# First heads loaded in fp32 and cast by VectorE, attention outputs copied out of PSUM at once, and zero matmuls without a bank of their own

## The chip, the cores and the metric

One core of a Trainium2 chip. The metric is the time of one execution in device microseconds (us); lower is better. Times are medians of several executions. A ratio is the mean time of one kernel's fast runs over the mean time of the other's fast runs of the same rounds on the same chip, so it is not quite the ratio of the medians quoted beside it. Profiles are of one execution each, and their span is about 1.8 us shorter than the time of the same execution.

## The reference

Eight batches, twelve heads, 448 rows, head width 64. Attention uses a sigmoid in place of the softmax; its output goes through a token mixer and a channel mixer with residuals.

```python
scores = scale * np.matmul(q, k.transpose(0, 1, 3, 2)) - np.log(S)
attn = 1.0 / (1.0 + np.exp(-scores))
x = np.matmul(attn, v)                       # then heads side by side: (8, 448, 768)
h = np.maximum(x.transpose(0, 2, 1) @ w_tok1, 0.0) @ w_tok2
u = x + h.transpose(0, 2, 1)
out = u + np.maximum(u @ w_ch1, 0.0) @ w_ch2
```

## The kernel before

The kernel is written as a plan. Every operation is declared with a guessed duration; a scheduler on the host picks an order for each engine from those guesses, and the instructions are emitted in that order. The order in each engine's list is then fixed, so a changed guess in one place can move instructions far away.

Batch 0 has a pipeline of its own, because nothing else can run yet: load q and k of four heads (a "unit", m = 0, 1, 2), turn them with TensorE transposes, score matmuls (qk), sigmoid on ScalarE, value matmuls (xa), copy to xT, transpose (xb), lay out as x, token mixer (k, then h), token result, eviction to uT. When all of uT is there, the first channel matmul (c<-uT) can start. From then on TensorE has work from the mixer of one batch and the attention of the next.

Loads cast fp32 to fp16 and are issued by GpSimd:

```python
for hs in [(0, 1)] if m or what == "v" else [(0,), (1,)]:
    def emit(hs=slice(hs[0], hs[-1] + 1)):
        for s in range(2):
            nc.gpsimd.dma_start(
                out=t[64 * s : 64 * s + 64, hs, :, :].rearrange("r h j e -> r h (j e)"),
                in_=view[s, :, hs, :],
            )
```

Zero matmuls keep TensorE occupied during the start-up. Nine come first ("up"), single ones ("fill") go where the plan sees TensorE idle between 4 and 21 us. All write one PSUM bank called idle:

```python
def run_up():
    for _ in range(9):
        nc.tensor.matmul(out=idle[:, :], lhsT=uT[0][:, 0, 0:128], rhs=uT[0][:, 0, :], start=True, stop=True)
# ...
def emit():      # a filler
    nc.tensor.matmul(out=idle[:, 0:256], lhsT=uT[0][:, 0, 0:128], rhs=uT[0][:, 0, 0:256], start=True, stop=True)
```

The token result of batch 0 is accumulated onto the attention output, which therefore stays in its PSUM banks until the end:

```python
nc.tensor.matmul(out=ps[s](every), lhsT=h1[0][...], rhs=w_tok2[:, t, 0:J, :],
                 start=False, stop=(t == 1), skip_group_check=True)
# ... and then one copy PSUM -> uT
```

## Time and profile before

Median 380.89 us (380.54 to 380.92, three runs).

| | before |
|---|---|
| span of the profile | 378.7 us |
| first score matmul, first sigmoid | 7.61, 8.03 us |
| end of batch 0's last sigmoid | 31.07 us |
| first channel matmul | 41.53 us |
| from there to the end | 337.2 us |

The page of the kernel before: the span, the share of the engines, and two rows of the table of 40 slices, one digit a slice (tenths of the slice that TensorE was busy, and tenths of full clock granted to it). PE is TensorE, PEld its weight loads, DVE VectorE, ACT ScalarE, POOL GpSimd; in the columns of the other views, L439 is line 439 of the kernel and a q after the name, as in SPq, is that engine's DMA queue.

```profile
span 378.7 us, 7932 instructions
PE 370.8 (98%) x3243; PEld 191.3 (51%) x3243; DVE 160.6 (42%) x296; ACT 205.7 (54%) x252; POOL 118.5 (31%) x265
...
PE   8999999999999999999999999999999999999994
...
PEclk9999999999999999999999999999999999999999
```

TensorE is the limit nearly everywhere. Its timeline at the start (columns: start in us, duration in us, engine, line, operation, output<-inputs, shapes, count):

```profile
1.16 3.54 PE L439 MATMUL idle<-uT 128*128 128x448 f16 x9 [1.16 <-DVE uT L432]
4.64 0.94 PE L499 MATMUL tk<-ident,k 128*64 128x128 f16 x7
5.51 0.61 PE L452 MATMUL idle<-uT 128*128 128x256 f16 x4
6.05 0.58 PE L499 MATMUL tq<-ident,q 128*64 128x128 f16 x7
6.56 0.61 PE L452 MATMUL idle<-uT 128*128 128x256 f16 x4
7.10 0.58 PE L499 MATMUL tk<-ident,k 128*64 128x128 f16 x7
7.61 0.57 PE L542 MATMUL qk<-qT,kT 64*64 64x448 f16 x4
```

The chain of waits of the kernel before, from batch 0's last sigmoid to the first channel matmuls (start, duration, what):

```profile
30.07 1.01 ACT attn L557
...
31.12 0.41 PE xa L579 x4
...
36.32 0.76 PE xa L693 x3
...
37.75 0.55 ACT uT L708
...
41.60 1.24 PE c L871 x6
```

So before 41.6 us the limit is the start-up chain, after it TensorE.

### The profile page before, as it was taken

Reading aid. Unit: us, or ns where it says so; the run is one execution under the profiler, and the core shown is the slowest. Engines: PE = TensorE matmul, PEld = TensorE weight load, DVE = VectorE, ACT = ScalarE, POOL = GpSimd, SP = SyncE. Lnnn points to the kernel's source line nnn. Section 1 sums busy time; section 2 is a strip of 40 time slices with the busy share of each in tenths; the row PEclk is TensorE's granted clock in tenths of the full one; section 3 lists DMA queues with packets and bytes.
Section 4 is the critical chain, followed back from the end, with each engine's and each line's share of the span. In section 5 each row is a group of like instructions: output and inputs, shape, how many; then the busy total and the mean of one; then the engine's idle time right before and its main releaser. Section 6 shows DMA issues by size and latency. Waiting matters only on the chain.

```text
span 378.7 us, 7932 instructions
## 1 busy us (share of the span) xinstructions
PE 370.8 (98%) x3243; PEld 191.3 (51%) x3243; DVE 160.6 (42%) x296; ACT 205.7 (54%) x252; POOL 118.5 (31%) x265
## 2 busy tenths in 40 slices
PE   8999999999999999999999999999999999999994
PEld 4555544555445554445444555444445655555662
DVE  3444434644344323453355313643432365754221
ACT  2987884486757766787678466846664130200000
POOL 9973326344344434444344343430000000000000
PEclk9999999999999999999999999999999999999999
DMA  6999999989987999999999999991103553300353
GB/s 80 181 176 205 208 210 176 153 141 184 146 126 111 174 162 235 146 120 208 190 149 161 162 180 156 145 197 39 30 16 97 113 106 94 73 2 0 85 123 85
DMA packets 98804, 50.56 MB, mean 134 GB/s; under 512 B 72336, under 2 KB 95120, under 8 KB 98768
## 3 DMA queue, kind: packets, MB, share of 16 engines
q0 software_dynamic: 24400, 21.93, 44.2%
q1 hardware_dynamic: 74368, 28.13, 40.8%
q8 instruction: 25, 0.41, 0.4%
q14 instruction: 11, 0.09, 0.1%
HBM read 43.84 MB, written 11.01 MB: 145 GB/s over the span
## 4 chain that ended last, share of the span: by engine, by line
PE 90%; POOL 4%; DMA 2%; ACT 1%; DVE 1%; issue 0%; POOLq 0%
PE c L871 30%; PE c L916 25%; PE qk L542 10%; PE xa L579 8%; PE yn L794 5%; PE k L764 5%; PE c L925 4%; DMA k<-in_k_dram 2%; POOL k L304 1%; POOL q L304 1%; POOL v L304 1%; ACT attn L557 1%; POOL w_tok L337 1%; PE xa L693 1%; PE tk L499 0%
## 5 line engine op out<-in xcount | busy, mean ns | idle before, releaser
L557 ACT ACTIVATE attn<-qk,att_bias 128x896 f16<-128x896 f32 (+1 forms) x172 | 160.9, 987 | 78.6 <-PE qk L542 78.3
L871 PE MATMUL c<-uT,w_ch 128*128 128x448 f16 x576 | 118.0, 353 | 0.1
L916 PE MATMUL c<-w_ch,h2aT 128*128 128x384 f16 x576 | 98.5, 326 | 0.0
L896 DVE TENSOR_SCALAR h2aT<-c 128x448 f16<-128x448 f32 x96 | 59.9, 624 | 77.4 <-PE c L871 77.2
L871 PEld LDWEIGHTS <-w_ch 128*128 128x128 f16 x576 | 53.4, 98 | 56.7 <-issue 11.6
L916 PEld LDWEIGHTS <-h2aT 128*128 128x128 f16 x576 | 55.2, 98 | 40.1 <-issue 4.5
L940 DVE TENSOR_TENSOR u<-u,c 128x384 f32<-128x384 f32 x48 | 26.6, 554 | 77.4 <-PE c L916 77.4
L542 PE MATMUL qk<-qT,kT 64*64 64x448 f16 x672 | 53.1, 363 | 0.2 <-ACT uT L708 0.2
L579 PE MATMUL xa<-attn,v 64*64 64x448 f16 x672 | 36.5, 350 | 0.4 <-ACT attn L557 0.4
L728 POOL COPY mark<-attn 1x1 f16<-1x1 f16 x54 | 9.6, 178 | 80.0 <-ACT attn L557 79.9
L823 ACT ACTIVATE u<-u 128x768 f16<-128x768 f32 x21 | 17.8, 846 | 25.0 <-DVE u L815 25.0
L542 PEld LDWEIGHTS <-kT 64*64 64x64 f16 x672 | 14.5, 104 | 29.8 <-issue 26.9
L815 DVE TENSOR_TENSOR u<-x,yn 128x384 f32<-128x384 f16 x48 | 24.9, 548 | 9.1 <-PE yn L794 9.1
L475 POOL COPY kp<-k 128x384 f16<-128x384 f16 (+1 forms) x54 | 21.2, 427 | 21.0 <-DMA k<-in_k_dram 16.0
L794 PE MATMUL yn<-h,w_tok 128*128 128x384 f16 x128 | 27.4, 328 | 0.0
L579 PEld LDWEIGHTS <-v 64*64 64x64 f16 x672 | 19.6, 107 | 13.2 <-issue 1.6
L612 ACT ACTIVATE xT<-xa 128x448 f16<-128x448 f32 x43 | 21.1, 547 | 9.3 <-PE xa L579 8.1
L475 POOL COPY qp<-q 128x384 f16<-128x384 f16 (+1 forms) x54 | 21.3, 430 | 9.0 <-DMA q<-in_q_dram 8.7
L764 PE MATMUL k<-x,w_tok 128*128 128x384 f16 x112 | 20.6, 327 | 0.1
L776 DVE TENSOR_SCALAR h<-k 128x384 f16<-128x384 f32 x28 | 15.4, 556 | 11.9 <-PE k L764 10.8
L315 POOL DMA_DIRECT2D k<-in_k_dram x21 | 15.0, 716 | 7.4 <-issue 5.9
L794 PEld LDWEIGHTS <-w_tok 128*128 128x128 f16 x128 | 11.0, 98 | 12.1 <-issue 5.9
(57 smaller groups left out, 186.7 us busy)
## 6 DMA issues: line engine op xcount, KB each, us to landing
out_dram<-u SPq DMA_DIRECT2D x48, 192.0 KB, 3.0
k<-in_k_dram POOLq DMA_DIRECT2D x21, 224.0 KB, 5.2
q<-in_q_dram POOLq DMA_DIRECT2D x21, 224.0 KB, 5.5
v<-in_v_dram POOLq DMA_DIRECT2D x21, 224.0 KB, 5.4
w_ch<-in_moe_w_ch_dram POOLq DMA_DIRECT2D x6, 768.0 KB, 15.9
out_dram<-ut SPq DMA_DIRECT2D x8, 192.0 KB, 3.2
v<-in_v_dram POOLq DMA_DIRECT2D x6, 112.0 KB, 4.7
x<-xT SPq DMA_TRANSPOSE x36, 4.6
```

The lines of the kernel that those rows point to most:

```text
L475: nc.gpsimd.tensor_copy(out=pm[:, to, :, :], in_=src[:, fr, :, :])
L542: nc.tensor.matmul(out=ps[64 * s : 64 * s + 64, h, 0:S], lhsT=kT[64 * h : 64 * h + 64, i, s, :], rhs=qT[64 * h : 64 * h + 64, :, s, :], st ...
L557: nc.scalar.activation(out=at[:, hs, :], in_=ps[:, hs, 0:S], func=SIGMOID, bias=bias_t[:, :], scale=att_scale,)
L579: nc.tensor.matmul(out=ps[s](slice(64 * h, 64 * h + 64)), lhsT=vf[64 * s : 64 * s + 64, h, order[i], :], rhs=attn[i][64 * s : 64 * s + 64, ...
L612: nc.scalar.activation(out=xt[:, s, c0 : c0 + S], in_=ps[s](every), func=COPYF)
L764: nc.tensor.matmul(out=ps[:, :], lhsT=w_tok1[:, w1_slot(side, blk), 128 * t : 128 * t + 128], rhs=X[b][:, x_block(side, blk), c], start=(b ...
L794: nc.tensor.matmul(out=ps[:, :], lhsT=w_tok2[:, t, s0 : s0 + 2, :], rhs=h1[b][:, t, c], start=(t == 0), stop=(t == 1),)
L815: nc.vector.tensor_tensor(out=to, in0=x, in1=y, op=ADD)
L871: nc.tensor.matmul(out=to(), lhsT=w_ch1[cb // 4][:, db, 128 * (cb % 4) : 128 * (cb % 4) + 128], rhs=uT[b][:, db, :], start=(db == 0), stop ...
L896: nc.vector.tensor_scalar(out=h2aT[b][:, cb, :], in0=to(), scalar1=0.0, scalar2=None, op0=MAX)
L916: nc.tensor.matmul(out=ps[:, :], lhsT=h2aT[b][:, cb, 128 * blk : 128 * blk + 128], rhs=w, start=(cb == 0), stop=(cb == NCB - 1),)
L940: nc.vector.tensor_tensor(out=t, in0=t, in1=ps[:, :], op=ADD)
```

## The change

Its intent is to reach the first channel matmul sooner. The first heads of q and k come as plain fp32 copies on the hardware queues of SP and ScalarE and are cast by VectorE, which saves two pairs of GpSimd issues and should start the sigmoids earlier. Batch 0's attention outputs are copied out of PSUM at once; the token result gets its own bank and VectorE adds x to it, so that banks come free and the units overlap. Fillers take a bank only for a moment. Around it: six zero matmuls at the start instead of nine, batch 1's keys and queries loaded ahead of the channel weights, batch 1's transposes no longer held back until batch 0's last uT evictions (`hold`), and evictions of the first two units that a late-bound variable had sent to ScalarE by mistake (`last` in a closure) back on VectorE. The core of the diff:

```diff
-    FILL = 21.0
+    FILL, UP = 21.0, 6
...
+                if m == 0 and hs == (0,):
+                    first = const(f"{what}_first", [128, J, E], FP32)
+                    def fetch(first=first):
+                        for s, queue in enumerate((nc.sync, nc.scalar)):
+                            queue.dma_start(
+                                out=first[64 * s : 64 * s + 64, :, :].rearrange("r j e -> r (j e)"),
+                                in_=view[s, :, 0, :],
+                            )
+                    def cast(first=first):
+                        nc.vector.tensor_copy(out=t[:, 0, :, :], in_=first[:, :, :])
+                    o = op(f"fetch_{what}", "SQ", 2.4 if what == "q" else 0.5, fetch, uses=[first])
+                    yield op(f"cast_{what}", "DVE", 0.32, cast, [o], [first, t], rank=-2)
+                    continue
...
-        for _ in range(9):
+        for _ in range(UP):
...
+        spot = bank(f"fill_{fill['n']}", [128, 256])
         def emit():
             nc.tensor.matmul(
-                out=idle[:, 0:256], lhsT=uT[0][:, 0, 0:128], rhs=uT[0][:, 0, 0:256], start=True, stop=True
+                out=spot[:, :], lhsT=uT[0][:, 0, 0:128], rhs=uT[0][:, 0, 0:256], start=True, stop=True
             )
...
-        hold = uT_ops[0][-2:] if b == 1 and m else []
+        hold = []
...
+                    tile_ = bank(f"kt_{b}_{m}_{s}", [128, S])
...
-                            start=False,
+                            start=(t == 0 and not last),
...
+                    if not last:
+                        nc.vector.tensor_tensor(out=y, in0=xt[:, s, 0:S], in1=to(every), op=ADD)
```

(Cut: the split of the first key eviction between ScalarE and VectorE, the table load moved ahead, load orders, priorities of the plan, a rule that holds token groups back when a value group is due.)

## The prediction

Short names in it: SWDGE are the loads that GpSimd issues, HWDGE those on the hardware queues of SP and ScalarE; K1 and KT are the two matmul steps of batch 0's token mixer; ch1_1 and ch1_2 are pieces of the channel weights.

> **What bounds it now.** From 41.6 us to about 346 us the chain of waits is almost nothing but matmul groups, and by the stage table TensorE is busy 29.2 of 29.3 us and then 100%: it is bound by TensorE there, and the change removes no real matmul from that stretch. What can be won lies in the start-up before the first channel matmul (41.6 us). The timeline shows three parts of it:
> 1. Filling: the first score matmul is at 7.61 us, the first sigmoid at 8.03. SWDGE issues of k/q (1.04 to 1.20 us a pair, one pair after another on GpSimd) land some 3.2 us after issue.
> 2. ScalarE: batch 0's sigmoids run from 8.03 to 31.08. They are worth about 20.7 us; 2.3 us go to waits and to other work on ScalarE (x evictions of 0.60, relus of 0.38).
> 3. Tail: last sigmoid 31.08 to last uT eviction 38.30, 7.2 us, strictly serial (xa, xT, xb, x, K1, h, KT, uT). Then 3.3 us of batch-1 transposes and scores.
>
> **What the change does.** The first q and k go in fp32 on SP and ScalarE queues; VectorE casts them. Two SWDGE pairs (2.24 us of GpSimd issue) disappear, so later loads are issued about 2.2 us earlier. The Trainium skill ("DMA: Bandwidth & Descriptors", SWDGE vs HWDGE) says a casting DMA must come from GpSimd, hence the VectorE cast. Its "Latency and other measured facts" gives 0.6 us to the first byte on hardware queues against 1 us; no load of this trace uses one, but output stores do: about 0.59 us to issue, 2.6 to 3.0 to land. ScalarE's own k issue stands behind the table load (1.28 us) and the tiny sigmoid, so I expect q landed at about 3.2 and k at 4 to 5.2, first score 5.5 to 6.5, first sigmoid about 6.2: gain 1.8 us.
>
> Batch 0's xa is copied out at once and the token result gets its own bank with x added on VectorE. By the instruction order, two x evictions (0.60 each), two relus and one uT eviction leave ScalarE. Estimate: sigmoids last 21.5 instead of 23.05 us; last one ends near 27.8. The tail stays about 7.3 us (the last unit is built as before), but batch 1's transposes are now inside it. First channel group at about 35.3 to 35.8 instead of 41.6, with two scores fewer done by then (about 0.7 us). So 6 − 0.7 ≈ 5.3 us, all on the critical path. Removed fillers (21 zero matmuls) filled idle slots: no gain.
>
> DMA is near saturation (1.25 of its share, 204 GB/s) from 28 to 60 us. Batch 1's six k/q loads now precede the first channel weight: 672 KB more, about 3.3 us at that rate, against 2.2 us earlier issue. I estimate it landed near 31 to 32 us, before 35; ch1_1 near 36, ch1_2 near 41, still ahead of use.
>
> **Prediction: 375.6 us** (1.4% faster), range 373.3 to 378.3. Faster by over 2%: 0.10; within 2%: 0.88; slower: 0.02.
>
> **What would show it.** Right: first sigmoid near 6.2 us; batch 0's last sigmoid near 28; first channel matmul near 35.5; from there to the end the same length as before (337 us) within 1 us.
>
> **What would make it wrong.** k on ScalarE's queue landing after 5.5 us; PE idle between the six zero matmuls and k, so the granted clock drops below 1.0 in the first slices; first channel matmul waiting for its weight or for batch 1's k/q (TensorE waits in order); VectorE, which takes over the work, delaying xT/h; or batch 1 becoming ScalarE-bound, so that the early start is given back before 70 us.

## The result, and the profile after

| | before | after |
|---|---|---|
| median | 380.88 us (six runs) | 382.38 us (380.96 to 383.12, six runs) |
| ratio | | 1.0036, 95% interval 1.0016 to 1.0056 |
| span of the profile | 378.7 us | 380.9 us |
| first sigmoid | 8.03 us | 7.53 us |
| end of batch 0's last sigmoid | 31.07 us | 32.92 us |
| first channel matmul | 41.53 us | 41.28 us |
| from there to the end | 337.2 us | 339.7 us |

The change did not gain 5.3 us; it lost about 1.5.

The page of the changed kernel, the same lines:

```profile
span 380.9 us, 7888 instructions
PE 370.5 (97%) x3222; PEld 189.2 (50%) x3222; DVE 163.0 (43%) x303; ACT 205.5 (54%) x249; POOL 115.4 (30%) x261
...
PE   6999999999999999999899999999999999999994
PEclk9599999999999999999999999999999999999999
```

The second slice of the clock row reads 5. The stage table shows it more closely (columns: stretch, its length, then busy us and number of instructions of PE, PEld, DVE, ACT and POOL, granted clock, DMA share, GB/s):

```profile
6.00:8.00 2.00, 1.50 (x22) 0.98 (x23) 1.29 (x3) 0.85 (x2) 2.00 (x5) 0.99 0.96 129
8.00:12.00 4.00, 4.00 (x43) 2.27 (x40) 1.79 (x3) 2.93 (x6) 3.89 (x7) 0.50 1.16 174
12.00:16.00 4.00, 4.00 (x32) 1.39 (x29) 1.09 (x2) 2.47 (x5) 3.12 (x7) 0.50 1.22 187
16.00:20.00 4.00, 4.00 (x39) 1.37 (x37) 0.11 (x1) 3.32 (x4) 2.79 (x5) 0.72 1.17 178
```

From about 8 to 18 us TensorE had half its clock. It reads as 100% busy there, but ScalarE (the fourth figure) is not: it waits for scores. The timeline of TensorE shows why the clock went, and what it cost:

```profile
1.17 2.42 PE L462 MATMUL idle<-uT 128*128 128x448 f16 x6 [1.17 <-DVE att_bias L273]
4.04 0.80 PE L526 MATMUL tq<-ident,q 128*64 128x128 f16 x7 [0.45 <-DVE q L317]
6.34 0.61 PE L526 MATMUL tk<-ident,k 128*64 128x128 f16 x11 [1.50 <-DVE k L317]
7.11 0.56 PE L576 MATMUL qk<-qT,kT 64*64 64x448 f16 x4 [0.16 <-ACT kT L543]
...
9.39 0.96 PE L526 MATMUL tk<-ident,k 128*64 128x128 f16 x14
```

The bracket is idle time before the row and what ended it. TensorE waits 0.45 us for the first queries and 1.50 us for the first keys, with no zero matmuls in these holes. The 14 transposes at 9.39 us take 0.96 us.

The keys are late because their transfers are. The view of the DMA issues (KB each, median us from issue to landing), of the first 60 us:

```profile
q_first<-in_q_dram SPq DMA_DIRECT2D x1, 112.0 KB, 2.5
q_first<-in_q_dram ACTq DMA_DIRECT2D x1, 112.0 KB, 2.8
k_first<-in_k_dram SPq DMA_DIRECT2D x1, 112.0 KB, 4.1
k_first<-in_k_dram ACTq DMA_DIRECT2D x1, 112.0 KB, 4.2
```

And there is a second, later loss. The waits of TensorE in the changed kernel (who waited for whom: us in total, times, longest us):

```profile
PE c L916 <- issue: 1.6, 1, 1.6
PE tk L526 <- DVE k L317: 1.5, 1, 1.5
```

The first line is one hole of 1.58 us at 184 us, ahead of batch 3's first channel group; the kernel before has none there. "issue" says that the profile saw no releaser. The operand that is then missing is uT of batch 3, which comes through transposing DMAs on SP's queue.

So there were two suspects: the clock in the start-up (theory A) and something later (rival B). The mean clock of the six runs spoke against A: the profiled one had 0.985 and took 382.74 us, but the others had 0.997 to 1.000 and took 380.96 to 383.12 us.

### The profile page after: what moved, and what is told of

Its sections match the earlier page's. It is cut to its first block, busy times and chain, and to the rows that moved or that the text cites. A ratio compares the mean times of both kernels' runs of the same rounds, so it can differ in the third digit from the quotient of the medians.

```text
span 380.9 us, 7888 instructions
## 1 busy us (share of the span) xinstructions
PE 370.5 (97%) x3222; PEld 189.2 (50%) x3222; DVE 163.0 (43%) x303; ACT 205.5 (54%) x249; POOL 115.4 (30%) x261
## 4 chain that ended last, share of the span: by engine, by line
PE 96%; DMA 1%; DVE 1%; issue 1%; ACT 0%; ACTq 0%; DVEq 0%
PE c L916 30%; PE c L961 25%; PE qk L576 12%; PE xa L614 9%; PE yn L839 6%; PE k L809 5%; PE c L970 4%; DMA k_first<-in_k_dram 1%; PE tk L526 1%; PE tq L526 1%; PE k L699 1%; PE xb L667 1%; PE fill L477 1%; PE kt L733 0%; PE ut L881 0%
## 5 line engine op out<-in xcount | busy, mean ns | idle before, releaser
L576 PE MATMUL qk<-qT,kT 64*64 64x448 f16 x672 | 54.4, 371 | 0.4 <-ACT uT L753 0.2
L614 PE MATMUL xa<-attn,v 64*64 64x448 f16 x672 | 37.6, 356 | 0.0
L336 POOL DMA_DIRECT2D q<-in_q_dram x21 | 15.1, 718 | 6.2 <-issue 5.6
```

Of the source, the lines that this page charges most:

```text
L576: nc.tensor.matmul(out=ps[64 * s : 64 * s + 64, h, 0:S], lhsT=kT[64 * h : 64 * h + 64, i, s, :], rhs=qT[64 * h : 64 * h + 64, :, s, :], st ...
L614: nc.tensor.matmul(out=ps[s](slice(64 * h, 64 * h + 64)), lhsT=vf[64 * s : 64 * s + 64, h, order[i], :], rhs=attn[i][64 * s : 64 * s + 64, ...
```

## The experiments

### Is it the clock?

**e1_again**: the changed kernel itself, for a second profile.

> The changed kernel as it is, for a second profile. Theory A (the clock of TensorE is halved for about 10 us in the start-up, because TensorE idles between the six zero matmuls and the late first keys): again matmul spacing at half speed before about 18 us, whatever mean clock the record prints; first channel matmul near 41 us; 381 to 383 us. Rival B (the clock in the first profile was an accident, and what eats the gain lies later, such as the 1.6 us wait of the first channel group of batch 3 at 184 us): a profile at full clock from 5 us on has its first channel matmul near 36 us and still ends at 381 to 383 us.

Measured 382.34 us; ratio 1.0028 (1.0002 to 1.0054). The record of this run prints a mean clock of 0.999 and 1.00 in every stage, and yet TensorE was at half speed:

```profile
8.00:12.00 4.00, 4.00 (x36) 2.14 (x34) 1.79 (x3) 2.46 (x5) 3.78 (x7) 1.00 1.14 166
```

The timeline of TensorE in e1_again:

```profile
10.21 0.96 PE L526 MATMUL tk<-ident,k 128*64 128x128 f16 x14
...
17.69 0.63 PE L614 MATMUL xa<-attn,v 64*64 64x448 f16 x8
18.25 0.28 PE L477 MATMUL fill<-uT 128*128 128x256 f16 x1
```

The same 14 transposes again take 0.96 us, and only from about 18 us on do matmuls come at full speed (one filler: 0.40 us at 13.38, 0.28 at 18.25). The trace holds clock records only from the first change on; here the first one is at about 18 us, and what lies before it is counted as full clock. In this run TensorE never had its full clock until then. So the mean clock cannot tell whether the start-up ran cold (at half clock); matmul durations can. First channel matmul at 41.62 us, as theory A says.

**e2_warm** and **e3_up13**: the changed kernel with the holes closed, in two ways. No other instruction moves.

```diff
 e2:     for _ in range(UP + 2):
 e2: +   for n in range(14 if zeros else 0):       # zeros: just before the first key transposes
 e2: +       nc.tensor.transpose(out=ps[0:64, n % 2, :, :], in_=uT[0][:, 0, 0:64], identity=ident[:, :])
 e3: -   for _ in range(UP):
 e3: +   for _ in range(UP + 7):
```

> Changed kernel with 8 instead of 6 zero matmuls at the start and 14 transposes of zeros (about 1.5 us) just before the first key transposes, in the slot in which TensorE waited for them; order of all else unchanged. Theory A: full clock from about 5 us, batch 0's last sigmoid ends near 28 instead of 32.9 us, first channel matmul near 36 instead of 41.3 us, time 376 to 378.5 us. Rival B: same time as the changed kernel, 381 to 383 us.

> Changed kernel with 13 zero matmuls at the start instead of 6 (TensorE busy until about 5.5 us, ahead of the query transposes, which makes those later by about 1.5 us). Theory A: no throttling either, first score at about 7.5 instead of 7.1 us but at full clock, time 376.5 to 379. Rival B: 381 to 383.

Measured 378.82 us, ratio 0.9935 (0.9905 to 0.9966), and 379.03 us, ratio 0.9954 (0.9913 to 0.9996), on the same chip and in the same rounds as e1_again. The timeline of TensorE in e3_up13:

```profile
1.17 4.20 PE L462 MATMUL idle<-uT 128*128 128x448 f16 x13 [1.17 <-DVE att_bias L273]
5.29 0.58 PE L526 MATMUL tq<-ident,q 128*64 128x128 f16 x7
6.34 0.61 PE L526 MATMUL tk<-ident,k 128*64 128x128 f16 x11 [0.47 <-DVE k L317]
...
9.04 0.58 PE L526 MATMUL tk<-ident,k 128*64 128x128 f16 x14
```

and of ScalarE in the same run:

```profile
7.53 16.17 ACT L592 ACTIVATE attn<-qk,att_bias 128x448 f16<-128x448 f32 x20 [0.47 <-PE qk L576]
```

The 14 transposes take 0.58 us instead of 0.96, and ScalarE runs 20 sigmoids without a hole. First sigmoid at 7.53 us, as in the changed kernel; last one ends at 29.16 instead of 32.92; first channel matmul at 37.52 instead of 41.28 us. Seven zero matmuls, which compute nothing, are worth 3.3 us here. Theory A holds: closing the holes keeps the clock up. Rival B, that the clock does not matter, falls. Not explained is how long the loss lasts: from 8 us on in the changed kernel, and from 6.34 us on in e1_again, TensorE has no hole longer than 0.2 us and yet stays at half clock until about 18 us. But the times lie a little over what I expected: the later loss is still there (a wait of 1.5 and 1.7 us).

**e4_before_bare**: the same lever on the kernel before, the other way round.

```diff
-        for _ in range(9):
+        for _ in range(6):
...
-        def emit():
+        def emit(n=fill["n"]):
+            if n < 10:
+                return
```

> The kernel before with 6 instead of 9 zero matmuls at the start and without the 8 zero matmuls between the first transposes, order of all else unchanged. Theory A: it idles in the same way and loses its clock too [...] between 5 and 18 us; 382 to 385 us. Rival B: those matmuls only filled idle slots, 380.5 to 381.5 us.

Measured 385.04 us, ratio 1.0080 (1.0037 to 1.0123). By count of the instructions ten fillers went, not eight, besides the three at the start. First sigmoid at 7.99 us as before, first channel matmul at 46.48 instead of 41.53 us. So the old fillers were not only idle time made busy: without them this kernel too runs cold, in this profile until about 23.3 us.

### The wait at 184 us

In SP's queue the last of batch 3's uT transposes stands behind the key transpose of batch 5 in the changed kernel and before it in the kernel before. In the plan of the changed kernel both become ready within 0.03 us of each other, so a small shift exchanges them. **e5_warm_swap** is e3_up13 with the two put back, **e6_cold_swap** the unmodified changed kernel with the same exchange.

```diff
             o = op(f"u16_{b}_{blk}", "ACT", 0.86, cast, adds, [u16, u[b], utile], rank=-2)
+            if (b, blk) == (3, 3):
+                next(x for x in plan.ops if x.name == "turnk_5_2").after.append(o)
```

Comparing the emitted lists shows that nothing else moves on any engine.

> The changed kernel with 13 zero matmuls at the start (as in the run before) and one exchange on the SP queue: the last transposing DMA of batch 3's u now goes before, not after, the transposing DMA of batch 5's last keys; no other instruction moves on any engine. Theory C (the wait of 1.6 to 1.7 us before batch 3's first channel group comes from that order, and is separate from the clock): the wait is gone, 377.0 to 378.0 us. Rival (DMA throughput is short at that point, and the order only decides who waits): a wait of similar size appears elsewhere on TensorE, 378.5 to 379.5 us.

> The changed kernel as it is (6 zero matmuls) with the same exchange on the SP queue alone. If clock and wait are independent terms: clock low in the start-up as in the changed kernel, first channel matmul at 41 to 42 us, no wait at 184 us, time about 1.6 us under the changed kernel: 380.3 to 381.3. If the low clock is all there is: 382 us.

e5_warm_swap: 378.33 us, ratio 0.9940 (0.9912 to 0.9968). SP's queue and TensorE in e3_up13:

```profile
174.16 1.72 SPq L503 DMA_TRANSPOSE kT<-kp  x1
175.97 1.21 SPq L896 DMA_TRANSPOSE uT<-u  x1
...
182.01 1.29 PE L916 MATMUL c<-uT,w_ch 128*128 128x448 f16 x6 [1.71 <-issue]
```

and in e5_warm_swap:

```profile
173.29 2.90 SPq L898 DMA_TRANSPOSE uT<-u  x2
176.29 1.24 SPq L503 DMA_TRANSPOSE kT<-kp  x1
...
180.87 1.31 PE L918 MATMUL c<-uT,w_ch 128*128 128x448 f16 x6
```

The wait is gone, and the largest new ones are two of 0.3 us. From the first channel matmul to the end e5 takes 338.4 us, e3 339.8. The time was a little above my range: in this profile the start-up was later by 0.64 us (first sigmoid 8.17). The 13 zero matmuls took 5.04 us there, against 4.20 in e3, because the clock rose later (the query transposes at 6.13 us still took 0.92 us); they ended at 6.2 us and so held up those transposes (5.29 us in e3), although the queries had been cast since 4.2. That the wait is gone is shown by the profiles (none in e5, 0.3 us in e11 below, against 1.5 and 1.7 in e2 and e3); the intervals of the two ratios overlap, so the times alone would not show it.

e6_cold_swap: 381.33 us, but its four runs spread from 377.39 to 382.76 and the ratio is 0.9992 (0.9934 to 1.005), so the time does not decide. Its profile shows a cold start-up (first channel matmul 41.19 us) and a wait of 0.4 us at that place. e1_again, with the order not exchanged, also had only 0.4 us. So in cold runs the wait itself varies from run to run, 0.4 to 1.6 us. One of the four runs, 377.39, would fit a start-up that happened to stay warm; that run has no profile, so this is a guess.

### Which half of the change carries the start-up gain?

**e7_loads_only**: the kernel before with the early fp32 loads (and 13 zero matmuls), meant to be these alone. **e8_psum_only**: the kernel before with the PSUM part alone (banks of its own for the token result, the four buffers for turned keys, fillers without a bank, evictions back on VectorE). **e10_rest**: e8 plus batch 1's keys and queries loaded first and their transposes no longer held back, so everything of the change's data flow but the early fp32 loads. The edits are parts of the diff above, but e7 holds more than its name and its text say: its kernel also has `hold = []`, so batch 1's transposes are no longer held back, and the split of the first key eviction. e10 adds to e8 (its text names the four buffers as well; e8 had them already):

```diff
-    load_all(1, 0)
-    ch1_ld.append(load_ch1(0))
-    ...
+    for m in range(NQ):
+        for what in ("k", "q"):
+            made = list(load_qkv(1, m, what))
+            loads[(1, m, what)][0].extend(made)
+    ...
-        hold = uT_ops[0][-2:] if b == 1 and m else []
+        hold = []
```

> The kernel before with only the early fp32 loads of the change (hardware queues, VectorE casts, order of the first transposes) and 13 zero matmuls so that the clock stays up; the token results still accumulate in the attention banks, batch 1's loads in the old order. First sigmoid at 7.5 us instead of 8.0 if the late second transfer is what holds it (first sigmoid 6.2 as predicted otherwise). I expect the last sigmoid of batch 0 near 30 us, first channel matmul near 40.5 us, 379.5 to 381 us: this half gives little by itself.

> The kernel before with only the PSUM part of the change (attention outputs copied out at once, token results in banks of their own, added by VectorE; zero matmuls hold no bank; evictions of the first units no longer fall to ScalarE), all loads as before and its 9 zero matmuls, so the clock stays up. If this half carries the gain: last sigmoid of batch 0 near 29.5 us, first channel matmul at 38.5 to 40 us, 378 to 380 us. If the early loads carry it: 380.5 to 381.5.

> Everything of the change but the early fp32 loads: the kernel before with the PSUM part of the earlier run and, added to it, batch 1's keys and queries loaded ahead of the channel weights, its transposes no longer held back behind batch 0's last results, and four buffers for turned keys. First loads and the 9 + 8 zero matmuls as before, so full clock. If the start-up gain needs these parts together and the early loads add little: first sigmoid 8.0 to 8.3, last one of batch 0 near 30, first channel matmul at 38 to 38.7 us (the warm changed kernel had 37.5 to 38.2), 378 to 380 us. If the early loads carry 1.8 us as predicted: 39.5 us or later.

| | first sigmoid | batch 0's last sigmoid ends | first channel matmul | time | ratio (95%) |
|---|---|---|---|---|---|
| before | 8.03 | 31.07 | 41.53 | 380.9 | |
| e7 loads, transposes not held | 8.26 | 30.34 | 39.6 | 383.07 | 1.0045 (1.0005 to 1.0085) |
| e8 PSUM part only | 8.30 | 30.29 | 41.0 | 380.81 | 0.9995 (0.9963 to 1.0027) |
| e10 all but the loads | 7.78 | 30.39 | 38.9 | 381.98 | 1.0035 (1.0012 to 1.0058) |
| e3 all of it, warm | 7.53 | 29.16 | 37.52 | 379.03 | 0.9954 (0.9913 to 0.9996) |

One run of e7 (387.94) counts as slow, because it is over 1.5% above the fastest, and is left out of its ratio, though not of the median in the table (382.38 without it). Its mean clock was 0.983 against 0.998 in the profiled run; that difference is worth, by my estimate, 0.015 of its span of 386.1 us, or 5.8 us, and it was 5.6 us slower, so a lost clock fits, but that run has no profile.

The early loads hardly make the first sigmoid earlier: it comes at 7.53 to 8.26 us in the profiles that have them beside the casting loads, and at 7.78 to 8.30 us in those that do not. In e5, e7 and e11, however, it is partly the 13 zero matmuls, ending at 6.2 us, that hold it at 8.17 to 8.26. The parts work together: 2.6 us of the 4.0 us of lead come without the early loads. The last 1.4 us go with them and with the rule named below, and their size is loose: the four warm profiles of the whole change have the first channel matmul at 37.52 to 38.46 us.

What the table shows besides is where the lead lies. From the last sigmoid to the first channel matmul it is 10.5 us in the kernel before and 10.7 in e8, which hold batch 1's transposes back, and 9.3, 8.5 and 8.4 us in e7, e10 and e3, which do not. No run releases the transposes alone, so this split is read from the profiles and not tested.

My expectation of e7 (379.5 to 381) and of e8 and e10 (378 to 380) failed in the total, and e8 at the first channel matmul too (38.5 to 40 expected): e7 and e10 have the lead and lose it later. Both are planned anew, and their first channel group of batch 1 starts at 92.9 us, later than the 91.6 of the kernel before and the 89.7 of e8. (All three leave out a rule of the change that holds token groups back when a value group is due.) Totals of such partial versions compare whole orders, not only the part that was changed; the milestones up to the first channel matmul are the fair comparison. What each later hole of these orders comes from I did not pursue. But one loss is again the clock. At 90 to 93 us e7 and e10 run the same instructions with the same holes (0.87, then 0.48 or 0.49, then 0.45 us). In e10's profile the clock is halved right after them, for 3.4 us from 92.9 us, and in e7's it is not. TensorE in e10_rest, then in e7_loads_only:

```profile
90.14 0.51 PE L848 MATMUL ut<-ident,u 128*128 128x128 f16 x6 [0.87 <-ACT u L835]
...
92.86 2.40 PE L883 MATMUL c<-uT,w_ch 128*128 128x448 f16 x6 [0.45 <-DVE uT L857]
```

```profile
90.21 0.51 PE L869 MATMUL ut<-ident,u 128*128 128x128 f16 x6 [0.87 <-ACT u L856]
...
92.93 1.29 PE L904 MATMUL c<-uT,w_ch 128*128 128x448 f16 x6 [0.45 <-DVE uT L878]
```

So the same holes can cost the clock in one execution and nothing in another.

### Why the keys land late

**e9_quiet**: e5_warm_swap with GpSimd's loads held back until the keys are there (two one-element copies on GpSimd that read the landed keys, then the loads).

> The exchanged and warm version with GpSimd's loads held until both halves of the first keys have landed, so that the four early fp32 transfers are alone on the DMA engines. Everything after is later by some 4 us and planned anew; only the landing counts here. Theory D (the first keys land at 5.6 us, 4.2 us after issue, because the casting loads that GpSimd issues from 1.45 us on share the 16 DMA engines): keys land at 3.9 to 4.5 us. Rival (the second transfer of a hardware queue is late by itself, or ScalarE's issue behind the table load is): still 5.4 us or later.

382.17 us. The keys landed 3.5 and 3.3 us after issue instead of 4.1 and 4.2:

```profile
k_first<-in_k_dram SPq DMA_DIRECT2D x1, 112.0 KB, 3.5
k_first<-in_k_dram ACTq DMA_DIRECT2D x1, 112.0 KB, 3.3
```

Their cast started at 4.88 us, 0.8 us sooner, and the first sigmoid came at 6.74 us. That is between my two brackets (landing at 4.8 us, against 3.9 to 4.5 and 5.4 or later): sharing the DMA engines with the casting loads explains 0.8 us; what makes the rest no run separates. The Trainium skill ("DMA: Bandwidth & Descriptors", Issuing engines are not separate DMA queues) says that DMAs of all issuing engines run on the same 16 engines and interleave; this run agrees. ScalarE's table load did not hold up the second issue: it was issued at 1.41 us, during the table load that began at 1.35.

### A version that beats both

**e11_steady**: e5_warm_swap with eight transposes of zeros in the last remaining hole before the keys.

> Candidate for the best version: the changed kernel with 13 zero matmuls, 8 transposes of zeros in the remaining wait for the first keys, and the exchange on the SP queue. I expect 377.5 to 378.5 us and fewer slow outliers than the version without the zero transposes (378.33, one run of four at 380.1): faster than before by 0.6 to 0.8%.

Measured 378.33 us (377.51 to 378.98, six runs); before 380.78 in the same rounds; ratio 0.9933 (0.9918 to 0.9948). It is a little faster than the kernel before, clear of noise though well under 2%, and its slowest run is faster than any of the kernel before. Its median is that of e5_warm_swap, so no gain of the zero transposes is shown; none of its six runs was as slow as the one of e5 at 380.11, which is too few runs to tell.

## Why the prediction was wrong

The predicted sequence was: first sigmoid 6.2, last sigmoid 27.8, first channel matmul about 35.5, then 337 us plus 0.7 for two scores not yet done. The profile of the changed kernel differs from that at four places, and they add up.

| step | predicted | measured | difference | shown by |
|---|---|---|---|---|
| first sigmoid | 6.2 us | 7.53 us | +1.3 | profile; 0.8 of it by e9_quiet |
| length of batch 0's sigmoids | 21.6 us | 25.4 us | +3.8 | e1 to e4: 21.6 us in e3, warm |
| last sigmoid to first channel matmul | 7.7 us | 8.4 us | +0.7 | profiles only: 8.4 us in e3 too |
| from there to the end | 337.9 us | 339.7 us | +1.8 | wait of 1.6 us; e5_warm_swap |

The sum is 7.6 us. Predicted −5.3 plus 7.6 gives +2.3, and the spans differ by +2.2 us.

- **The step that failed.** "Removed fillers (21 zero matmuls) filled idle slots: no gain." I counted the zero matmuls as costless and so their removal as neutral. They held TensorE's clock up. Taken away, TensorE ran at half speed until 18 us, the sigmoids waited for scores, and 3.8 us were lost. I had named a lower clock among the things that could make the prediction wrong, "in the first slices", but gave it no time in the sum. e2 and e3 put the clock back and won 3.3 to 3.5 us of time over e1 in the same rounds; e4 took it from the kernel before and lost 3.7.
- **The first sigmoid.** The mechanism I feared, ScalarE's issue behind the table load, did not happen. The size was off because I took the landing time of output stores, 2.6 to 3.0 us, for four transfers that share the engines with each other and with GpSimd's; it was 4.1 to 4.2.
- **Right in the middle.** With the clock up, the sigmoids take the predicted 21.6 us, which supports the reading that ScalarE lost time to evictions that did not belong there. The relief without the early loads is real, but little of it is the PSUM part alone: the first channel matmul comes 0.5 us earlier in e8 and 2.6 us earlier in e10, which adds the new load order and the released transposes.
- **The tail.** I said that batch 1's transposes would now be inside it for nothing. From last sigmoid to first channel matmul it fell from 10.5 to 8.4 us, not to the 7.7 I predicted; in e3 it is 8.4 as well. The chain of waits shows transposes on TensorE between its steps; no run tests this, so it is argued only.
- **"From there to the end the same length".** Wrong by 1.8 us. Two orders that look alike differ in which of two transposing DMAs goes first. Exchanging just these two removes the wait in a warm run (e5). In cold runs the wait was 1.6 us once and 0.4 us once without an exchange, so its size there is a matter of timing between runs.
- **Weights.** The channel weights did not hold up the first channel matmul, as predicted.

The Trainium skill ("TensorE: Matmul & The Clock Gate", What's actually happening) describes two clock states, half and full, set from activity in free-running windows of 3.4 us, with half as the default. The recorded states are 1.0 and 0.5, and the half-speed stretch of the first profile, 8.0 to 18.2 us, is 10.24 us long, three such windows. A free-running window also fits that runs of one kernel differ (e6: 377.4 to 382.8) and that the same holes halved the clock in e10 and not in e7, though only the profiled runs were checked. That the half speed lasted three windows in which TensorE shows no hole does not follow from this, and stays open. Its advice to avoid idle gaps over about 3 us ("Why this matters for your kernels") was too weak for this kernel: the longest gap before the drop was 1.50 us. Nor does the length of a gap decide alone: the 1.58 us at 184 us cost the changed kernel no clock.

## What to carry to other kernels

Before removing work that computes nothing from an engine whose clock depends on activity, time the same instruction early and late in the trace; if it takes 0.96 us in one place and 0.58 in another, the idle slots were not free. Close the holes that a faster start opens (here seven zero matmuls were worth 3.3 us) before judging the change, but no further than the data's arrival: in e5 they ran 2 us past the cast of the queries. And where a planner orders the engines, compare the emitted orders after every change: two transfers that tie in the plan may swap and cost 1.6 us in a place that the change never touched.

## What the Trainium skill lacked or had wrong

- "TensorE: Matmul & The Clock Gate" (Why this matters for your kernels) warns of idle gaps over about 3 us. Here the clock dropped with no gap longer than 1.50 us (0.45 and 1.50 us idle between 3.6 and 6.3 us), after one window of full clock, and stayed at half for 10.24 us while TensorE read as 100% busy. In e10_rest it dropped after holes of at most 0.87 us, in e9_quiet after one of 0.99 us; after the 1.58 us at 184 us in the changed kernel it did not. (Elsewhere the page tells of short idle stretches that make the clock oscillate, without a length.)
- The same page (Seeing it yourself) says that clock records are unreliable. It lacks the way in which they misled here: nothing is recorded before the first change, so a run that was at half speed until about 18 us printed a mean clock of 0.999. Matmul durations showed it (14 transposes in 0.96 us against 0.58).
- The same page puts the warm-up at about 3.4 us of activity and advises not to fit it. In e1_again TensorE was in use from 1.16 us, without a hole over 0.2 us from 6.34 us, and at full speed only from about 18 us; in e3_up13, with the holes closed, already at 5.3 us (7 transposes in 0.58 us).
- "DMA: Bandwidth & Descriptors" (Latency and other measured facts) gives about 0.6 us to the first byte on hardware queues. That alone led to nothing usable here: loads of 112 KB landed 2.5 to 2.8 us after issue, and the second pair, issued right after it, 4.1 to 4.2 us (3.3 to 3.5 with the casting loads held back). The page's fit for a whole transfer is for GpSimd's path, and it has none for a second transfer behind a first.
